# DMA transposes, 64-row tail matmuls, one merged broadcast and GpSimd weight loads in a fused attention and mixer kernel

## The chip, the cores and the metric

The kernel runs on one core of one Trainium2 chip. The metric is the device time of one execution in microseconds (us); lower is better. Times quoted for a kernel are medians of its runs. The median of the kernel before was 252.76 us in its three first runs. A profiled execution has a "span", which is about 2 us shorter than its time. TensorE's clock is granted by a throttle, so every run also has a mean granted clock (1.0 is full speed). A run more than 1.5% above the fastest of its kernel is called slow and is kept out of every ratio.

Engines are named as in the profile: PE is TensorE's matmul, PEld its weight load, DVE is VectorE, ACT ScalarE, POOL GpSimd, SP SyncE, and a "q" behind a name is that engine's queue of issued transfers.

## The reference

Two blocks follow each other over x of shape 1 x 2048 x 448, all in bf16. The first is sliding-window attention (16 heads of 28, a window of 8 keys at a distance of 2). The second mixes neighbouring tokens and ends in an MLP of width 1792.

```python
def _A_ref(x, wqkv, wo):                     # x is layernorm(x)
    q, k, v = split_heads(x @ wqkv)          # cut
    ...                                      # 8 keys at distance 2, softmax over them
    return o @ wo
def _B_ref(x, w1, w2, w3, w4):               # x is layernorm(h)
    h = _gelu(_layernorm(x) @ w1)
    hs = shifted_quarters(h) @ w2            # cut: four quarters shifted by -1, +1, -2, +2 tokens
    x1 = x + hs
    return x1 + _gelu(_layernorm(x1) @ w3) @ w4

h  = x + _A_ref(_layernorm(x), wqkv, wo)
h2 = h + _B_ref(_layernorm(h), w1, w2, w3, w4)
```

## The kernel before

A small scheduler takes a list of operations, works out the dependences, and gives each engine one fixed order. Within an engine that order is then kept, whatever happens at run time. The 2048 tokens are handled in four stages of 512. The phases of a stage are A1 (layernorm), QK, V, att (scores, exp, mask, values), WO, B1, B2, W3 and B3.

Every layernorm output (512 tokens x 448) has to be turned so that the 448 channels lie on partitions. TensorE does this in 16 transposes of 128 x 112, and a copy of 1024 columns per half brings the result back from PSUM:

```python
KC = 112                                     # 448 = 4 x 112
def transposes(ls, dst):
    for half in range(2):
        T = tile()
        for il in range(4):
            for cc in range(2):
                c = 2 * half + cc
                S.add("pe", "transpose", 64.0, out=T(...), in_=lntm[:, ls, il, c*KC:(c+1)*KC], identity=ident[:])
        copy(dst(half), T(...), 1024, 0.52)
```

A contraction over 448 channels is four passes of 112 rows. The largest is W3, 14 output tiles of 4 matmuls each:

```python
def phase_W3(g):
    ...
    transposes(ls, lambda half: actT[:, a, 2*half:2*half+2, :])
    for f in range(NF):                      # 14
        T = tile()
        for c in range(4):
            mm(T(...), w3_s[:, c, f*128:(f+1)*128], actT[:, a, c, :], c == 0, c == 3, 512)
        act(h3T[g % 2][:, f, :], T(...), ACT.Gelu_apprx_tanh, 512)
```

At the end of an attention stage the softmax sums are gathered, inverted, stored to a scratch in HBM and broadcast back. Each of four rows of 8 KB goes to 32 partitions. VectorE then multiplies four tiles, oT, by the result:

```python
def phase_att(t):
    ...                                      # scores, exp, masks, values -> osb
    for j in range(4):
        dma("zg%d_%d" % (par, j), zp[32*j:32*j+32, par, :], osb[32*j+28:32*j+29, ...])
    dve("reciprocal", 400, out=rzp[:, par, :], in_=zp[:, par, :])
    ...
    dma("zs%d" % par, zd..., rzp[:, par, :], 32768)
    for j in range(4):
        dma("zb%d" % j, rzb[32*j:32*j+32, :, :]..., bass.AP(rz_d, (4*t+j)*2048, [[0, 32], [1, 2048]]), 32*8192)
    for c in range(4):
        dve("tensor_tensor", 512, out=oT[:, par, c, :], in0=osb[:, par, c, :], in1=rzb[:, c, :], op=ALU.mult)
```

All weights are loaded on SyncE's queue at the start, and every normalisation runs on VectorE.

## Time and profile before

| | before |
|---|---|
| median time, four runs beside the changed kernel | 252.35 us |
| span of the profiled run | 250.6 us |
| TensorE busy | 224.6 us (90%) |
| first QK matmul starts | 10.4 us |
| last value matmul of attention starts | 105.0 us |
| last B1 matmul of the last stage starts | 141.9 us |
| last B3 matmul starts | 245.4 us |

These are lines from the profile page of the kernel before: the busy times of the engines; the busy tenths of TensorE, its granted clock in tenths and the DMA share in 40 slices of the span; the chain that ended last, by engine; and the broadcast's transfers with the size of each and the median time to landing.

```profile
PE 224.6 (90%) x1681; PEld 112.9 (45%) x1681; DVE 138.2 (55%) x306; ACT 120.7 (48%) x175; POOL 46.2 (18%) x71
...
PE   0799799999979998898995999899998999899992
...
PEclk9999659999965995589998899999999999999998
DMA  6999900070610052007000000000100000000111
...
PE 72%; DVE 16%; ACT 5%; POOL 2%; issue 2%; DVEq 0%
...
rzb<-rz_scratch SPq DMA_DIRECT2D x16, 256.0 KB, 4.4
```

TensorE is the limit: busy for 90% of the span, and 72% of the chain. Among its groups of instructions the 192 transposes are 18.8 us, with 11.2 us of idle just before them. The slices show the few places where it rests and its clock drops: the start and the starts of attention stages. The DMA row shows that nearly all loads happen in the first five slices (about 31 us); later there is only the traffic of the broadcasts and outputs.

The next lines are from the timeline of TensorE (start us, busy us, engine, line, operation, tiles, count). The first two make one batch of 16 transposes, and the last is one W3 group of 56 matmuls:

```profile
159.62 0.58 PE L1100 MATMUL ps<-ident,lntm 128*112 128x128 bf16 x6
160.90 0.77 PE L1100 MATMUL ps<-ident,lntm 128*112 128x128 bf16 x10 [0.70 <-DVE lntm L1100]
...
162.45 12.25 PE L1100 MATMUL ps<-actT,w_s 112*128 112x512 bf16 x56
```

With the wait in its middle this batch ends 2.05 us after it starts; a batch without a wait takes about 1.06 us. A W3 group takes 12.25 us, 0.22 us a matmul.

Finally, a line of VectorE's timeline: the four multiplies of the last attention stage, which use a broadcast that SyncE issued at 113.58 us:

```profile
123.49 2.49 DVE L1100 TENSOR_TENSOR oT<-arena,rzb 128x512 bf16<-128x512 f32 x4
```

### The profile page before, as it was taken

How to read it: one execution, taken by the hardware profiler on the slowest of the kernel's cores; microseconds unless marked ns; L12 is line 12 of the kernel's file. 1: busy time of each engine (PE TensorE's matmuls, PEld its weight loads, DVE VectorE, ACT ScalarE, POOL GpSimd, SP SyncE). 2: the span in 40 equal slices, each digit the busy share in tenths (PEclk: the TensorE clock that was granted, in tenths of full speed). 3: DMA queues.
4: the chain of work that ended last, by engine and by line, in shares of the span. 5: the costliest groups of instructions: out<-in, count | busy, mean ns of one | idle time of the engine just before them, and what ended most of it. 6: DMA issues, size and time to landing. Idle time of an engine off the chain costs nothing.

```text
span 250.6 us, 4082 instructions
## 1 busy us (share of the span) xinstructions
PE 224.6 (90%) x1681; PEld 112.9 (45%) x1681; DVE 138.2 (55%) x306; ACT 120.7 (48%) x175; POOL 46.2 (18%) x71
## 2 busy tenths in 40 slices
PE   0799799999979998898995999899998999899992
PEld 0336345645533556354544533533554345533550
DVE  7596862595785677877999602700385008700220
ACT  2468836896485649645422575166002740156000
POOL 8512200010031003003017200800016000710000
PEclk9999659999965995589998899999999999999998
DMA  6999900070610052007000000000100000000111
GB/s 164 291 222 232 275 12 5 8 171 5 146 29 0 8 131 44 3 7 173 0 1 3 0 0 0 21 18 0 36 15 25 0 16 23 20 18 0 42 39 42
DMA packets 11696, 14.07 MB, mean 56 GB/s; under 512 B 2136, under 2 KB 10712, under 8 KB 11160
## 3 DMA queue, kind: packets, MB, share of 16 engines
q1 hardware_dynamic: 11672, 13.75, 22.7%
q8 instruction: 15, 0.25, 0.4%
q14 instruction: 9, 0.07, 0.1%
HBM read 11.65 MB, written 1.97 MB: 54 GB/s over the span
## 4 chain that ended last, share of the span: by engine, by line
PE 72%; DVE 16%; ACT 5%; POOL 2%; issue 2%; DVEq 0%
PE ps L1100 72%; DVE st L1100 4%; DVE lntm L1100 4%; ACT pt L1100 3%; DVE xb L1100 2%; POOL rstd L1100 2%; DVE mv L1100 1%; DVE oT L1100 1%; ACT hT L1100 1%; ACT actT L1100 1%; DVE pt L1100 1%; ACT arena L1100 0%; POOL vtmp L1100 0%; DVE xin L1100 0%; DVE msk L1100 0%
## 5 line engine op out<-in xcount | busy, mean ns | idle before, releaser
L1100 PE MATMUL ps<-actT,w_s 112*128 112x512 bf16 (+1 forms) x288 | 64.2, 382 | 1.2 <-DVE mv L1100 1.1
L1100 ACT ACTIVATE arena<-ps 128x512 bf16<-128x512 f32 (+1 forms) x67 | 40.0, 597 | 28.0 <-PE ps L1100 27.8
L1100 PE MATMUL ps<-w_s,arena 128*128 128x448 bf16 x224 | 43.9, 353 | 0.0
L1100 PEld LDWEIGHTS ps<-actT,w_s 112*128 112x128 bf16 (+1 forms) x288 | 25.9, 106 | 37.8 <-ACT arena L1100 15.2
L1100 PE MATMUL ps<-hT,arena 112*128 112x512 bf16 x128 | 39.4, 453 | 0.5 <-ACT hT L1100 0.2
L1100 DVE TENSOR_TENSOR ost<-ps,xb 128x448 bf16<-128x448 f32 x16 | 10.0, 622 | 54.2 <-PE ps L1100 54.1
L1100 ACT ACTIVATE pt<-ps 110x1024 bf16<-110x1024 f32 x32 | 30.3, 1030 | 7.8 <-PE ps L1100 7.8
L1100 ACT ACTIVATE actT<-ps 112x1024 bf16<-112x1024 bf16 x10 | 10.0, 1028 | 44.2 <-PE ps L1100 44.2
L1100 POOL TENSOR_SCALAR vtmp<-mv 128x4 f32<-128x4 f32 (+1 forms) x19 | 4.6, 241 | 143.0 <-DVE mv L1100 142.3
L1100 PEld LDWEIGHTS ps<-w_s,arena 128*128 128x128 bf16 x224 | 21.5, 98 | 20.5 <-DVE xb L1100 0.6
L1100 PE MATMUL ps<-ident,lntm 128*112 128x128 bf16 x192 | 18.8, 250 | 11.2 <-DVE lntm L1100 11.2
L1100 PEld LDWEIGHTS ps<-ident,lntm 128*112 128x112 bf16 x192 | 15.9, 152 | 14.5 <-DVE lntm L1100 12.1
L1100 DVE TENSOR_TENSOR pt<-pt,msk 110x1024 bf16<-110x1024 bf16 x32 | 21.0, 684 | 1.7 <-ACT pt L1100 1.7
L1100 DVE BATCH_NORM_STATS2 st<-xin 128x6 f32<-128x448 bf16 x32 | 19.2, 601 | 2.4 <-DMA xin<-in_A_x_dram 1.9
L1100 PEld LDWEIGHTS ps<-hT,arena 112*128 112x128 bf16 x128 | 11.6, 108 | 17.9 <-issue 6.0
L1100 POOL TENSOR_TENSOR rstd<-vtmp,mhalf 128x4 f32<-128x4 f32 (+1 forms) x19 | 18.5, 972 | 1.6
L1100 POOL TENSOR_TENSOR xb<-xb,xin 128x448 bf16<-128x448 bf16 x16 | 16.7, 1072 | 1.5 <-DVE lntm L1100 1.5
L1100 DVE TENSOR_TENSOR xb<-ps,xb 128x448 bf16<-128x448 f32 x16 | 9.6, 600 | 13.4 <-PE ps L1100 13.1
L1100 PE MATMUL ps<-qT,kT 28*110 28x103 bf16 (+1 forms) x320 | 13.2, 229 | 3.8 <-ACT pt L1100 3.5
L1100 PE MATMUL ps<-wo_s,oT 128*128 128x448 bf16 x64 | 16.2, 403 | 0.4 <-DVE oT L1100 0.3
L1100 PE MATMUL ps<-arena,hT 112*110 112x448 bf16 x80 | 15.8, 353 | 0.0
L1100 ACT ACTIVATE gT<-ps 112x512 bf16<-112x512 f32 x16 | 9.6, 600 | 12.3 <-PE ps L1100 12.3
(52 smaller groups left out, 188.5 us busy)
## 6 DMA issues: line engine op xcount, KB each, us to landing
rzb<-rz_scratch SPq DMA_DIRECT2D x16, 256.0 KB, 4.4
w_s<-in_B_w_dram SPq DMA_DIRECT2D x2, 1568.0 KB, 18.0
out_dram<-ost SPq DMA_DIRECT2D x16, 112.0 KB, 1.7
xin<-in_A_x_dram SPq DMA_DIRECT2D x3, 448.0 KB, 8.9
arena<-in_A_wqkv_dram SPq DMA_DIRECT2D x3, 392.0 KB, 6.2
w_s<-in_B_w_dram SPq DMA_DIRECT2D x2, 392.0 KB, 10.5
xin<-in_A_x_dram SPq DMA_DIRECT2D x4, 112.0 KB, 2.2
wo_s<-in_A_wo_dram SPq DMA_DIRECT2D x4, 98.0 KB
```

The costliest lines, as they stand in the source:

```text
L1100: inst = getattr(eng, op.meth)(**op.kw)
```

## The change

The intent is to take work off TensorE: 11 of the 12 batches of transposes go to the DMA, and a contraction over 448 becomes three passes of 128 rows and one of 64, where the 64-row passes ("tails") of two output tiles use the two halves of the array side by side. To match this, layernorm outputs are padded to 512 columns (the last 64 repeated), and the last 64 rows of weights are loaded twice. Beside it, the four broadcast transfers are merged into one, the four gathers into one, the weights move to GpSimd's queue and are issued at two later points, the normalisations may run on VectorE or ScalarE (ScalarE needs a second quantity, nmr, made by two more GpSimd instructions), and some late phases change places. The diff, cut to its core:

```diff
+    def dmaw(chan, out_ap, in_ap, nbytes):
+        return S.add("pool", "dma_start", 1100.0, chan=chan, lat=nbytes, out=out_ap, in_=in_ap)
 ...
     def normalize(slot, kind, i, out_ap, in_ap):
-        S.add("dve", "tensor_scalar", 390, ...)
+        S.add("flex", "tensor_scalar", 0, ..., opts={"dve": ("tensor_scalar", ...), "act": ("activation", ...)})
 ...
+    def transpose_dma(ls, a, b, dst):
+        S.add("sp", "dma_start_transpose", 500.0, chan="tr%d_%d" % (ls, a), lat=(b - a) * 128 * 1024, out=dst,
+              in_=lntm[:, ls, a:b, :].rearrange("p i n -> p (i n)"))
+
+    def mm_k(outs, lhs, rhs, n):
+        for g, o in enumerate(outs):
+            for c in range(3):
+                mm(o, lhs(g, c, 0, 128), rhs(g, c, 0, 128), c == 0, False, n)
+        for g, o in enumerate(outs):
+            r = 64 * (g % 2)
+            S.add("pe", "matmul", n / 4.8 + 8, out=o, lhsT=lhs(g, 3, r, r + 64), rhs=rhs(g, 3, r, r + 64), start=False, stop=True)
 ...
-        for j in range(4):
-            dma("zb%d" % j, rzb[32 * j:32 * j + 32, :, :].rearrange("p c n -> p (c n)"),
-                bass.AP(rz_d, (4 * t + j) * 2048, [[0, 32], [1, 2048]]), 32 * 8192)
+        dma("zb", rzb[:].rearrange("p c n -> p (c n)"), bass.AP(rz_d, 4 * t * 2048, [[2048, 4], [0, 32], [1, 2048]]), 128 * 8192)
 ...
-        transposes(ls, lambda half: actT[:, a, 2 * half:2 * half + 2, :])
-        for f in range(NF):
-            T = tile()
-            for c in range(4):
-                mm(T(lambda p: p[:, 0, :]), w3_s[:, c, f * 128:(f + 1) * 128], actT[:, a, c, :], c == 0, c == 3, 512)
-            act(h3T[g % 2][:, f, :], T(lambda p: p[:, 0, :]), ACT.Gelu_apprx_tanh, 512)
+        transpose_dma(ls, 0, 4, actT[:, a, :, :, :].rearrange("p i c n -> p (i c) n"))
+        for f0 in range(0, NF, 2):
+            Ts = [tile(), tile()]
+            mm_k([T(lambda p: p[:, 0, :]) for T in Ts], ...)
+            for q, T in enumerate(Ts):
+                act(h3T[g % 2][:, f0 + q, :], T(lambda p: p[:, 0, :]), ACT.Gelu_apprx_tanh, 512)
 ...
+    behind(load_attn_out)        # after A1 1: w_o, w1, w2
 ...
+    behind(load_mlp)             # after A1 2: w3, w4
 ...
-    phase_WO(3)
     phase_B1(0)
     phase_B1(1)
     phase_B2(0)
+    phase_WO(3)
```

## The prediction

> **What bounds the kernel now.** TensorE. The page gives it 224.6 us of a 250.6 us span (90%), and 72% of the chain that ended last (VectorE 138.2, ScalarE 120.7). TensorE's idle 26 us lies in the first 7 us, in short waits at the start of attention stages (the timeline: 0.3 to 0.5 us before each group of score matmuls, for an exp), and at hand-overs of normalised tiles (the waits: 11.2 us for lntm, 7.0 of it the start). The granted clock is 0.57 to 0.59 in three stretches of 10 to 13 us after such waits.
>
> **Removed.** (1) 176 of 192 TensorE transposes. A batch of 16 takes about 1.06 us in the timeline, so 11 batches are 11.7 us, plus about 4 us of idle before them. (2) The half-row tails. A full 512-column matmul takes 0.218 us at full clock (26 in 5.78 us). If two 64-row tails run side by side, 3.5 passes for 4 save 28 of them in W3 (6.1 us), 8 in W1 (1.7), 16 in QK (3.5), and 8 narrower ones in V (1.5): 12.8 us. The trace supports this: 30 score matmuls of 28 rows and 103 columns on alternating row groups took 0.71 us, 24 ns each.
>
> Gross: 28 us, nearly all on the chain.
>
> **Added.** (a) A DMA transpose of 512 KB where a 1.06 us batch stood. At 261 GB/s (the Trainium skill, "DMA: Bandwidth & Descriptors", latency and other measured facts) this is 2 us; with the 1.9 us a small transfer here needs to land, and its issue, I estimate 5 to 6 us. No trace shows one yet. (b) Two more small GpSimd instructions per statistics step; in the first stage four steps are in series on the chain: about +2 us. (c) The reciprocal's broadcast becomes one 1 MB transfer instead of four of 256 KB (4.4 us to landing). Its source's outermost dimension is 4. The same page (how many engines) says such a transfer uses 4 engines. With 8 KB packets at 0.31 us or more that is 32 in a row: about 10 us, landing near 12 us (estimate).
>
> **Where the gain is lost.** After the last attention stage, reciprocal, store, broadcast (12 us) and four multiplies (2.5 us) make a chain of about 20 us to WO 3, while TensorE has some 10.5 us of other work: a wait of about 9 us. Then WO 3, statistics, transpose, B1 3: again up to 5 us. In attention, all four stages now start with 80 or more score and value matmuls without filler: one more cold stretch (about 5 us) and 3 to 4 us of waits, against 11 us saved. The final stretch (W3 and B3, 108.4 us in before) keeps its gain: about 13 to 14 us.
>
> Sum: start +2, attention -3, middle 0, end -13.
>
> **Predicted time:** 240 us, 228 to 252 in 8 of 10 cases. Faster by over 2%: 0.76; within 2%: 0.18; slower: 0.06.
>
> **What will show it.** TensorE busy near 200 us, W3 plus its tails near 10.7 us a group; transposes landing in 4 to 7 us; broadcast landing near 12 us; a wait of 5 to 10 us in front of WO 3; four cold stretches; first QK matmul near 12.3 us instead of 10.4.
>
> **What would make it wrong.** DMA transposes of 10 us or more each put waits before B1 and W3 and could cost all the gain. Tails that do not run side by side lose 12 us. If the broadcast still lands in 5 us, the time falls toward 232.

## The result, and the profile after

The changed kernel took 299.46 us in the median of four runs (298.64 to 303.14; the last of these is a slow run), against 252.35 us (251.75 to 252.82) before. The ratio is 1.186, with a 95% interval of 1.180 to 1.192: 47 us slower. A ratio is always the mean time of one kernel's fast runs over that of the other's fast runs in the same rounds, so it is not quite the ratio of the medians quoted.

The lines of the profile page and, for the two kinds of transpose, of the list of transfers, which answer to those shown of before:

```profile
PE 221.0 (74%) x1499; PEld 96.6 (33%) x1505; DVE 130.9 (44%) x289; ACT 122.0 (41%) x187; POOL 61.7 (21%) x121
...
PE   0596399890097909986596048699999999999992
...
PEclk9999589577569775966579659799999999999998
...
PE 45%; DMA 33%; DVE 10%; SPq 4%; POOL 3%; issue 2%; ACT 1%; POOLq 0%
...
rzb<-rz_scratch SPq DMA_DIRECT2D x4, 1024.0 KB
```

```profile
hT<-lntm SPq DMA_TRANSPOSE x12, 2.5
...
actT<-lntm SPq DMA_TRANSPOSE x8, 4.3
```

The chain that ended last is no longer TensorE's: its share fell from 72% to 45%, and DMA, which was absent, has 33%. The row of TensorE has holes of whole slices (each is 7.4 us) in the first 60% of the span, and its clock row has many more fives, sixes and sevens. The DMA transposes landed in 2.5 us (128 KB) and 4.3 us (512 KB), no slower than predicted. These are medians, counted from the start of the issue. One transpose of 20 was far slower: it was issued at 163.86 us, while the last broadcast was in flight, and took 9.5 us to issue and 11.6 us to land.

The waits of the changed kernel (who waited for whom: total us, times, longest us):

```profile
DVE oT L1167 <- DMA rzb<-rz_scratch: 45.4, 4, 17.2
...
PE ps L1167 <- DVE oT L1167: 18.9, 2, 13.3
...
PE ps L1167 <- DVE qT L1167: 14.9, 1, 14.9
...
PE ps L1167 <- DVE pt L1167: 9.2, 3, 8.5
```

VectorE waited for the broadcast in all four stages, 45.4 us together. TensorE then waited for VectorE: for oT, which needs the broadcast, but also for qT and pt, which do not. Waits of TensorE for DMA transposes are small beside these: 4.2 us once for hT and 2.2 us once for actT. The timeline of VectorE in the first attention stage shows why:

```profile
60.28 1.28 DVE L1167 TENSOR_TENSOR pt<-pt,msk 110x1024 bf16<-110x1024 bf16 x2
...
78.74 2.50 DVE L1167 TENSOR_TENSOR oT<-arena,rzb 128x512 bf16<-128x512 f32 x4 [17.18 <-DMA rzb<-rz_scratch]
81.16 0.68 DVE L1167 CAST qT<-ps 128x512 bf16<-128x512 f32 x1
```

VectorE's next operation in its order was oT, so it stood still for 17.18 us. The copy of qT, whose input was long there, sat behind it. TensorE needed the PSUM bank which that copy frees:

```profile
81.90 6.62 PE L1167 MATMUL ps<-arena,hT 128*110 128x448 bf16 x20 [14.95 <-DVE qT L1167]
```

The chain that ended last (start us, us, what) shows what the broadcast costs, from its issue to its use. These are its lines for the first and the last stage:

```profile
50.74 27.98 DMA rzb<-rz_scratch
78.74 2.50 DVE oT L1167 x4
...
156.25 17.45 DMA rzb<-rz_scratch
```

The two stages between have 17.81 and 18.64 us. That is 17.5 to 28 us from issue to use. In the kernel before, the four transfers together take 6.6 to 6.8 us from the first issue to the last landing (one alone 4.4 us in the median). In the last stage TensorE waited 13.28 us in front of WO 3, where the prediction had about 9:

```profile
174.47 5.76 PE L1167 MATMUL ps<-wo_s,oT 128*128 128x448 bf16 x16 [13.28 <-DVE oT L1167]
```

### The profile page after: what moved, and what is told of

Read it like the earlier page. It is cut to its first block, busy times and chain, and to the rows that moved or that the text cites. A ratio compares the mean times of both kernels' runs of the same rounds, so it can differ in the third digit from the quotient of the medians.

```text
span 296.8 us, 3753 instructions
## 1 busy us (share of the span) xinstructions
PE 221.0 (74%) x1499; PEld 96.6 (33%) x1505; DVE 130.9 (44%) x289; ACT 122.0 (41%) x187; POOL 61.7 (21%) x121
## 4 chain that ended last, share of the span: by engine, by line
PE 45%; DMA 33%; DVE 10%; SPq 4%; POOL 3%; issue 2%; ACT 1%; POOLq 0%
PE ps L1167 45%; DMA rzb<-rz_scratch 28%; SPq L1167 4%; DVE oT L1167 3%; DMA rz_scratch<-rzp 2%; DVE st L1167 2%; DMA actT<-lntm 1%; DMA hT<-lntm 1%; DVE lntm L1167 1%; POOL rstd L1167 1%; DVE xb L1167 1%; POOL nmr L1167 1%; ACT lntm L1167 1%; POOL msk L1167 1%; DVE mv L1167 1%
## 5 line engine op out<-in xcount | busy, mean ns | idle before, releaser
L1167 PE MATMUL ps<-actT,w_s 128*128 128x512 bf16 (+3 forms) x288 | 68.2, 405 | 2.8 <-DMA actT<-lntm 2.2
L1167 ACT ACTIVATE arena<-ps 128x512 bf16<-128x512 f32 (+1 forms) x67 | 37.0, 595 | 59.8 <-PE ps L1167 59.7
L1167 PE MATMUL ps<-hT,arena 128*128 128x512 bf16 (+1 forms) x122 | 36.4, 463 | 5.5 <-DMA hT<-lntm 4.2
L1167 PEld LDWEIGHTS ps<-actT,w_s 128*128 128x128 bf16 (+3 forms) x288 | 24.6, 108 | 44.9 <-issue 25.8
L1167 PE MATMUL ps<-wo_s,oT 128*128 128x448 bf16 x64 | 18.6, 442 | 19.1 <-DVE oT L1167 18.9
L1167 PE MATMUL ps<-arena,hT 128*110 128x448 bf16 (+1 forms) x80 | 19.5, 406 | 14.9 <-DVE qT L1167 14.9
L1167 DVE TENSOR_TENSOR oT<-arena,rzb 128x512 bf16<-128x512 f32 x16 | 10.0, 687 | 45.4 <-DMA rzb<-rz_scratch 45.4
L1167 PEld LDWEIGHTS ps<-hT,arena 128*128 128x128 bf16 (+1 forms) x128 | 10.4, 105 | 24.4 <-issue 13.2
L1167 PE MATMUL ps<-qT,kT 28*110 28x103 bf16 (+1 forms) x320 | 13.8, 236 | 5.9 <-ACT pt L1167 5.6
L1167 PE MATMUL ps<-pt,vt 110*32 110x103 bf16 (+1 forms) x320 | 9.9, 263 | 10.4 <-DVE pt L1167 8.9
L1167 PEld LDWEIGHTS ps<-arena,hT 128*110 128x110 bf16 (+1 forms) x80 | 9.1, 140 | 25.4 <-DVE qT L1167 15.2
```

The costliest lines, as they stand in the source:

```text
L1167: inst = getattr(eng, op.meth)(**op.kw)
```

## The experiments

Theories A to C stood at the outset for the 47 us. Theory D was added after the first four runs, for what was left:

- A: the merged broadcast runs on few engines and its lateness blocks VectorE's queue in every stage.
- B: the DMA transposes, with their small packets, slow every other transfer.
- C: the weight loads, now on GpSimd's queue and in the middle of attention, slow every other transfer.
- D: the 64-row tails do not save what they should.

All experiments are judged by ratio to the fast runs of the unchanged kernel before on the same chip. The batches ran on different chips, so two experiments are compared by these ratios.

| experiment | median us | ratio to before (95%) |
|---|---|---|
| e1: after, broadcast in four transfers | 258.08 | 1.025 (1.018 to 1.032) |
| e2: before, broadcast in one transfer | 287.59 | 1.136 (1.127 to 1.146) |
| e3: after, one transfer with 16 rows outermost | 264.05 | 1.046 (1.039 to 1.054) |
| e4: after, one transfer with 8 rows outermost | 271.91 | one run |
| f1: e1, tails of a pair on the same rows | 265.92 | 1.054 (1.047 to 1.061) |
| f2: e1, tails four by four in W1 and W3 | 252.62 | 0.999 (0.994 to 1.004) |
| f3: e1, four full passes instead of tails | 248.99 | 0.984 (0.978 to 0.989) |
| f5: e1, full-row tails in the same order | 256.90 | 1.020 (1.013 to 1.026) |
| g1: e1, all transposes on TensorE | 251.60 | 0.994 (0.987 to 1.001) |
| h1: e1, weights on SyncE's queue | 256.25 | 1.007 (1.000 to 1.015) |
| h2: e1, normalise on VectorE only | 255.15 | 1.011 (1.003 to 1.019) |
| c1: f3 and g1 together | 253.97 | 1.010 (1.005 to 1.015) |
| b1: f3, but W3 as in f2 | 254.23 | 1.014 (1.005 to 1.023) |
| b2: b1 with an early start as before | 247.82 | 0.988 (0.980 to 0.995) |
| b5: before with late changes only | 243.01 | 0.968 (0.959 to 0.976) |

Where a median includes slow runs (h1 above all, two of four), the ratio is the better guide.

### Is it the broadcast? e1, e2, e3, e4

**e1** is the changed kernel with the one broadcast issued as the four transfers of before, at the same place and with the same semaphore. The order of operations on every engine is the same as in the changed kernel (the traces agree; SyncE alone has more issues).

```diff
-dma("zb", rzb[:]..., bass.AP(rz_d, 4*t*2048, [[2048, 4], [0, 32], [1, 2048]]), 128*8192)
+for j in range(4):        # one entry for the scheduler, four transfers when emitted
+    dma(rzb[32*j:32*j+32, :, :]..., bass.AP(rz_d, (4*t + j)*2048, [[0, 32], [1, 2048]]))
```

> The changed kernel with only the reciprocal's broadcast split again into four transfers of 256 KB (each with an outermost source dimension of 32); every engine's order stays as in the changed kernel. Theory A (the 1 MB transfer runs on 4 DMA engines because its outermost source dimension is 4, and the multiplies that need it block VectorE's in-order queue): landing falls from 17 to 28 us to 5 to 7 us, VectorE's 45 us of waiting for it nearly vanish, the time falls to 232 to 248 us. Theory B (the new transposes, 23552 packets of 256 B on the same queue, slow the broadcast) and theory C (the weights on the GpSimd queue slow it): the bytes and the company are the same, so landing stays above 12 us and the time above 285 us.

Measured: 258.08 us, so this one split takes back 41 of the 47 us (1.186/1.025 is 1.157). The rest is still slower than before, and the absolute time came out above the range that my theory gave it. A line of its waits, to be compared with that of the changed kernel above:

```profile
DVE oT L1171 <- DMA rzb<-rz_scratch: 3.9, 2, 3.1
```

VectorE's wait for the broadcast went from 45.4 to 3.9 us, and in the same view TensorE's waits for qT and for pt fell from 14.9 and 9.2 us to 0.9 and 0.3. Theories B and C cannot explain the 41 us, since transposes and weight loads are untouched here.

**e2** is the counterpart: the kernel before with nothing but the merge. Only SyncE's list of issues changes.

```diff
-for j in range(4):
-    dma("zb%d" % j, rzb[32*j:32*j+32, :, :]..., bass.AP(rz_d, (4*t+j)*2048, [[0, 32], [1, 2048]]), 32*8192)
+dma("zb", rzb[:]..., bass.AP(rz_d, 4*t*2048, [[2048, 4], [0, 32], [1, 2048]]), 128*8192)
```

> The kernel before with only its four broadcast transfers made one of 1 MB with an outermost source dimension of 4; no DMA transpose, no weight on the GpSimd queue, same order on TensorE, VectorE, ScalarE and GpSimd. Theory A: landing 15 to 19 us, about 4 packets of 8 KB in flight, the time rises by 25 to 45 us to 278 to 298 us. Theories B and C: landing stays near 5 us and the time within 2% of before.

Measured: 1.136 in fast runs, 34 us slower than before. Neither a transpose on the DMA nor a moved weight load is in this kernel. The wait of VectorE (the profiled run was a slow one, so its absolute times are not compared closely):

```profile
DVE oT L1098 <- DMA rzb<-rz_scratch: 39.3, 4, 11.6
```

**e3 and e4** keep one transfer of 1 MB, but change the size of the source's outermost dimension. The scratch gets four (e3) or two (e4) copies of each row, and the broadcast reads 16 rows for 8 partitions each, or 8 rows for 16 each.

```diff
-dma("zs%d" % par, zd..., rzp[:, par, :], 32768)
-dma("zb", rzb[:]..., bass.AP(rz_d, 4*t*2048, [[2048, 4], [0, 32], [1, 2048]]), 128*8192)
+for u in range(4):                                   # e4: 2
+    dma(bass.AP(rz_d, (16*t + u)*2048, [[8192, 4], [64, 32], [1, 64]]), rzp[:, par, :])
+dma("zb", rzb[:]..., bass.AP(rz_d, 16*t*2048, [[2048, 16], [0, 8], [1, 2048]]), 128*8192)   # e4: [2048, 8], [0, 16]
```

> The changed kernel with the broadcast still one transfer of 1 MB, but the scratch holds every reciprocal row four times, so that the outermost source dimension is 16 (four small stores of 32 KB instead of one). Theory A: about 16 packets in flight, landing 5 to 7 us, time within 2% of the run with four transfers (232 to 250 us). If instead merging into one instruction is what hurts: landing stays near 17 us and the time near 295 us.

> As the 16-row run but every row twice: outermost source dimension 8. Theory A: about 8 packets in flight, landing 8 to 10 us, time between the 16-row run and the changed kernel, 240 to 265 us. If the engine count is not what matters: landing near 17 us or near 5 us as the other runs, not between.

Measured: 264.05 us with 16 rows and 271.91 us with 8. Both are above their expected ranges, but their order is right: the more rows outermost, the faster. VectorE's wait, first for e3, then for e4:

```profile
DVE oT L1171 <- DMA rzb<-rz_scratch: 9.8, 3, 9.3
```

```profile
DVE oT L1171 <- DMA rzb<-rz_scratch: 21.8, 4, 11.5
```

The trace also has every 8 KB packet of these transfers. For each of the four stages, in order, the mean number of packets in flight and the time from the first to the end of the last packet, worked out from the 128 packets of SyncE's queue that follow each issue:

| kernel | outermost rows | in flight | us from first to last packet |
|---|---|---|---|
| before (four transfers) | 32 each | 14.2, 14.8, 14.9, 15.0 | 5.0, 4.8, 4.9, 5.1 |
| after | 4 | 2.7, 3.9, 3.7, 3.7 | 22.8, 15.9, 16.7, 15.5 |
| e2 | 4 | 3.5, 3.8, 3.7, 3.7 | 16.6, 16.4, 18.2, 16.8 |
| e4 | 8 | 5.8, 7.6, 7.5, 8.1 | 12.2, 9.0, 9.6, 9.4 |
| e3 | 16 | 13.8, 14.7, 14.7, 15.3 | 5.3, 4.9, 4.9, 5.3 |
| e1 (four transfers) | 32 each | 8.2, 14.9, 14.9, 14.8 | 8.8, 5.0, 5.0, 5.1 |

Four rows outermost give on average up to 4 packets in flight, 8 give about 8, 16 give about 15. The Trainium skill says this in "DMA: Bandwidth & Descriptors", section "Why a DMA increments its semaphore by 16 and not by 1": a transfer goes to the largest number of engines, up to 16, that divides the slowest dimension of both access patterns. The trace agrees, with 3.9 in flight on average at most for 4 rows (6 for moments). Theory A is shown: the same merge of four transfers into one costs 41 us with 4 rows outermost, but with 16 rows the broadcast is as quick as four transfers.

What remains beside it lies in the first stage. Four weight loads were issued there on GpSimd's queue, between 49.6 and 53.8 us in after, e1, e3 and e4. The first broadcast of e1 takes 8.8 us, and the first packets of those of after, e1 and e4 come 4 to 5 us after the issue, against 0.9 to 1.4 us in their later stages. In e3 the broadcast itself takes 5.3 us, but it was issued only at 64.7 us, behind four small stores issued at 50.2 to 52.0 us, for which SyncE waited 12.2 us; the longest wait of e3, 9.3 us, is in this stage. These runs alone do not say why; the weights loaded at that time are a likely reason (see h1 and b1).

### What do the 64-row tails save? f1, f2, f3, f5

All of these start from e1.

**f1** lets both tails of a pair use the same 64 rows (in V, W1 and W3), so that they have to run one after the other.

```diff
-            r = 64 * (g % 2)
+            r = 0                    # V, W1, W3; QK as it was
```

> The changed kernel with the four broadcast transfers, and with every 64-row tail matmul of V, W1 and W3 on rows 0 to 63 (before, the two of a pair used rows 0 to 63 and 64 to 127). Same order on all engines, same result. Theory D (the tails of a pair do run side by side, 4 ns apart, but the switches from 128 rows to 64 and back each expose a weight load of about 0.1 us, so the pair costs as much as two full passes): the tails now run one after the other, so a group of 56 W3 matmuls goes from 12.1 us to 17 or 18 us if each tail costs a further 0.2 us, and the kernel gets 6 to 10 us slower. Theory E (the tails never overlapped): no change, 12.1 us a group, time within 1% of the run with four transfers.

**f2** takes four tiles at once in W1 and W3, so that two pairs of tails follow each other and a W3 group of 14 tiles changes between 128 and 64 rows and back 4 times instead of 7.

```diff
-        for f0 in range(0, NF, 2):
-            Ts = [tile(), tile()]
+        for f0 in range(0, NF, 4):
+            Ts = [tile() for _ in range(min(4, NF - f0))]      # W1: one group of four
```

> The changed kernel with the four broadcast transfers and W1 and W3 computed in groups of four tiles (twelve full passes, then four tails) instead of two, so that there are half as many switches. Theory D: about 0.2 us less per four tiles, a group of 56 W3 matmuls falls from 12.1 us to 11.3 to 11.6 us, the kernel 2 to 4 us faster than with pairs (254 to 256 us). Theory E: 12.1 us stays.

**f3** gives up tails: every tile gets four full passes of 128 rows, with the second half of the last chunk of weights set to zero.

```diff
-            for c in range(3):
-                mm(o, lhs(g, c, 0, 128), rhs(g, c, 0, 128), c == 0, False, n)
-        for g, o in enumerate(outs):
-            r = 64 * (g % 2)
-            S.add("pe", "matmul", n / 4.8 + 8, ..., start=False, stop=True)
+            for c in range(4):
+                mm(o, lhs(g, c, 0, 128), rhs(g, c, 0, 128), c == 0, c == 3, n)
```

> The changed kernel with the four broadcast transfers and four full passes of 128 rows (the last chunk's rows 64 to 127 of the weights are zero) instead of three and a half: undoes that part of the change on TensorE. Theory D: a W3 group takes 12.0 to 12.2 us as with the tails, and the time is within 1% of the run with four transfers (255 to 261 us). My prediction on record, that the half passes save 12.8 us, would have this kernel at about 270 us.

**f5** makes the tails 128 rows deep at the very places where the 64-row tails stood (QK keeps its 64 rows), with the order of e1 on every engine. Its result is wrong (relative error 0.31), since the last 64 channels are then counted twice.

```diff
-            r = 64 * (g % 2)
-            S.add(..., lhsT=lhs(g, 3, r, r + 64), rhs=rhs(g, 3, r, r + 64), ...)
+            r, k = (0, 128)          # V, W1, W3
+            S.add(..., lhsT=lhs(g, 3, r, r + k), rhs=rhs(g, 3, r, r + k), ...)
```

> The changed kernel with the four broadcast transfers, with the last chunk's matmuls of V, W1 and W3 as full 128-row passes in the same places; every engine's order stays exactly as in the run with four transfers. The result is wrong on purpose (the last 64 rows count twice), the work is that of four full passes. Theory D (the half-row pairs save next to nothing because of the two switches): within 1% of the run with four transfers, 256 to 260 us, a W3 group 11.85 us start to start against 11.74. Then the 9 us that the kernel with four full passes gained came from the order and from tiles finishing one at a time, not from the matmuls. If full passes are themselves what is faster: 248 to 251 us.

Measured: the timeline of TensorE has one W3 group in each of e1, f1, f2 and f3, in this order. The kernel before had 12.25 us for the same group.

```profile
178.61 12.12 PE L1171 MATMUL ps<-actT,w_s 128*128 128x512 bf16 x56 [0.51 <-DVE ost L1171]
```

```profile
181.60 13.60 PE L1171 MATMUL ps<-actT,w_s 128*128 128x512 bf16 x56 [0.49 <-DVE ost L1171]
```

```profile
175.41 11.48 PE L1171 MATMUL ps<-actT,w_s 128*128 128x512 bf16 x56 [0.52 <-DVE ost L1171]
```

```profile
170.31 12.25 PE L1173 MATMUL ps<-actT,w_s 128*128 128x512 bf16 x56 [0.52 <-DVE ost L1173]
```

Three and a half passes cost 12.12 us, four full ones 12.25 us. Predicted were 10.7. In f1 the group grew by 1.48 us, which is 7 tails of 0.21 us, so in e1 the tails of a pair do run side by side. (My expectation of 17 to 18 us for that group had the size wrong.) The saving is lost around them. The single records of one pair in e1, from the trace (start us, ns, what):

```
182.915 379 MATMUL     128 rows
183.131 379 MATMUL     128 rows      the last full pass, 0.216 after the one before
183.439  92 LDWEIGHTS   64 rows
183.442  92 LDWEIGHTS   64 rows
183.443 386 MATMUL      64 rows      0.312 after the last full pass
183.446 386 MATMUL      64 rows      0.003 after its partner
183.760  96 LDWEIGHTS  128 rows
183.765 390 MATMUL     128 rows      0.319 after the tails
183.991 379 MATMUL     128 rows      0.226 after that
```

The second tail starts 3 ns after the first. But the step into the tails takes 0.312 us and the step out of them 0.319, where a step between full passes takes about 0.22. The other pairs of W3 in e1 agree: 0.311 or 0.312 us in, 3 or 4 ns between the tails, 0.318 or 0.319 us out, with three steps that were longer. From the start of the last full pass to that of the next one it is 0.634 us. With two full passes in place of the pair, these would be three steps of 0.216, or 0.648 us (worked out). In the timeline of the weight loads in e1 the same is seen as a gap labelled "issue" before both:

```profile
181.19 0.10 PEld L1171 LDWEIGHTS ps<-actT,w_s 128*128 128x128 bf16 x1
181.72 0.10 PEld L1171 LDWEIGHTS ps<-actT,w_s 64*128 64x128 bf16 x2 [0.42 <-issue]
182.04 0.55 PEld L1171 LDWEIGHTS ps<-actT,w_s 128*128 128x128 bf16 x4 [0.23 <-issue]
```

The 64-row weights are loaded only 0.308 us after the last full pass has started, and the next 128-row weights 0.314 us after the tails. Between full passes the loads hide under the running matmuls. The Trainium skill, "TensorE: Matmul & The Clock Gate", section "Part 3: Packing small matmuls — row/col tiling", gives about 4 ns from one packed tile to the next, and says that the load of a tile is pulled ahead of running matmuls where the row groups do not conflict. The first agrees with these records: 3 ns between the tails. The second only in part: no load was early where a half and the full array follow each other, but full passes use the same rows too and their loads are early (the section also names a background weight buffer). Why the switch stops the early load is not shown here. f2 has 3 switches in and out fewer a group and gains 0.64 us, 0.21 us each: this is the same cost again, seen from the other side. As a kernel f2 is some 6 us faster than e1 (0.999 against 1.025), more than its expectation of 2 to 4 us and more than the 2.6 us of four W3 groups; what else it gains is open, as with f3.

Now the surprise: f3, whose matmuls are no cheaper, is 9 us faster than e1, and f5, which keeps e1's order, is only some 1 us faster. So f3's gain hardly comes from the matmuls of V, W1 and W3. QK, which f5 left at 64 rows, is no cheaper in f3 either where it can be compared: the 32 QK matmuls of the first stage take 7.88 us from the first start to the last in e1 and 8.29 us in f3. What is left is what the two differ in otherwise: the places and the pairing of the tiles. In f3 each tile ends by itself and its copy can start, and the scheduler arranges all engines anew. Which of these it is, and how much belongs to the tail loads of weights that f3 also drops, is left open.

### The DMA transposes: g1, c1

**g1** is e1 with all transposes back on TensorE, writing the layout of the changed kernel. **c1** is g1 and f3 together.

```diff
-        transpose_dma(ls, 0, 4, actT[:, a, :, :, :].rearrange("p i c n -> p (i c) n"))
+        transposes(ls, lambda half: actT[:, a, :, 2*half:2*half+2, :].rearrange("p i c n -> p c i n"))
```

> The changed kernel with the four broadcast transfers and all transposes back on TensorE (with the 512-column layout and the half-row tails). If the DMA transposes are a gain (my prediction: 11.7 us of TensorE work and some 4 us of idle saved), this is 8 to 14 us slower than the run with four transfers, 266 to 272 us. If the waits they bring (4.5 us at the first, 2.3 us before B1 3, and the cold clock after them) eat that gain, it is within 1.5%, 254 to 262 us.

> The changed kernel with the four broadcast transfers, four full passes and all transposes on TensorE: what is left of the change is the order of the phases, the GpSimd queue and the choice of engine for normalising. If the two undone parts each cost what they showed alone (9 us and 6.5 us) and add up: 240 to 246 us. If both only disturb the same schedule: 247 to 253 us, as each alone or as before. If the rest of the change is worth nothing or harms: 252 to 258 us.

Measured: g1 0.994, faster than both of its expected ranges. So in e1's surroundings the kernel is 3% slower with the DMA transposes than without (1.025/0.994), though they take 11 batches from TensorE; g1's order is the scheduler's own as well, so the 3% are not the transposes' alone. c1 is 1.010: the two gains over e1, 3% from g1 and 4% from f3, do not add but cancel in part. This is in the last of its three expected ranges, and it suggests that a part's worth depends on the order that the scheduler makes around it. Why TensorE does not profit is plain in one place. The transpose is longer than what it replaces, and where the next matmul needs it at once, TensorE waits. A line of the TensorE timeline of e1, at the first matmul of the second stage:

```profile
36.01 0.63 PE L1171 MATMUL ps<-hT,arena 128*128 128x512 bf16 x1 [4.53 <-DMA hT<-lntm]
```

Four transposes of 128 KB are issued in series, each about 1.27 us (5.27 us for the four in the changed kernel, from 26.93 us on), and then the last lands. TensorE waited 4.5 us for them. In the kernel before one batch took 1.06 us. This one wait is shown; what the other transposes cost or save in e1 was not separated.

### Weights and normalisation: h1, h2

**h1** is e1 with the weights on SyncE's queue, at the same points of the program. **h2** is e1 with normalisation on VectorE alone and without the two extra GpSimd instructions.

```diff
     def dmaw(chan, out_ap, in_ap, nbytes):
-        return S.add("pool", "dma_start", 1100.0, chan=chan, lat=nbytes, out=out_ap, in_=in_ap)
+        return S.add("sp", "dma_start", 500.0, chan=chan, lat=nbytes, out=out_ap, in_=in_ap)
```

> The changed kernel with the four broadcast transfers and the weight loads issued on the SyncE queue instead of the GpSimd queue, at the same points of the program. GpSimd loses 8.5 us of issuing between the statistics of the third and fourth stage. If the GpSimd queue costs nothing on the chain: within 1.5%, 254 to 262 us; if its loads delay statistics or share the broadcast's time (the first broadcast took 12.5 us beside them, the others 5), up to 6 us faster, 251 to 255 us.

```diff
-        pool("tensor_scalar", 60, out=nmr..., scalar1=-1.0, ...)
-        pool("tensor_tensor", 60, out=nmr..., in1=rstd..., op=ALU.mult)
 ...
-        S.add("flex", "tensor_scalar", 0, ..., opts={"dve": ..., "act": ...})
+        S.add("dve", "tensor_scalar", 390, ..., op0=ALU.subtract, op1=ALU.mult)
```

> The changed kernel with the four broadcast transfers, normalising on VectorE alone and without the two extra GpSimd instructions per statistics step. The first QK matmul comes 2 to 2.5 us earlier (10.4 us as in before, against 12.8). If that is all: 254 to 257 us. If ScalarE's normalises (0.75 us where VectorE takes 0.39) and the GpSimd steps also sit on later chains: 248 to 254 us.

Measured: h1 1.007 and h2 1.011, against e1's 1.025. Both seem to undo a part of what was left, 1.8% and 1.4%; h1 rests on two fast runs, and h2's interval touches that of e1. The profiled runs of both were slow ones, so only the ratios are used, and one plain reading: in h2 the first QK matmul starts at 10.6 us (12.8 in e1, 10.4 before). That the place of the weight loads, in the middle of attention, costs something is likely but was not isolated: no run has them at the start again with the rest of the change kept.

### Toward a faster kernel: b1, b2, b5

**b1** is f3, but W3 keeps 64-row tails in groups of four, as in f2. **b2** is b1 with the first two stages transposed on TensorE, and the first stage normalised without nmr.

```diff
-        for f0 in range(0, NF, 2):                 # f3
-            Ts = [tile(), tile()]; mm_k(...)
+        for f0 in range(0, NF, 4):                 # b1
+            Ts = [tile() for _ in range(min(4, NF - f0))]; mm_half(...)
 ...
-        if t == 0:                                 # b1
+        if t <= 1:                                 # b2
             transposes(...)
```

> The changed kernel with the four broadcast transfers, full passes for QK, V and W1, and half-row tails only in W3 in groups of four tiles. The kernel with full passes everywhere had 0.984 of the time before; this should take 2.6 us off (11.10 for 11.87 us a group), 244 to 249 us. If the pairing of tiles hurts in W3 as well: 249 to 254 us.

> As b1, with the second stage's transposes on TensorE too (the first DMA transpose made TensorE wait 4.5 us) and without the extra GpSimd steps in the first stage. If these two are the costs of the attention part: first QK matmul at 10.5 us, no wait for hT, 4 to 6 us faster than b1, 239 to 245 us. If the gain is taken by other waits in the attention stages: within 2 us of b1.

Measured: b1 1.014, slower than f3 instead of faster: a miss. Its W3 groups did take the 11.10 us of f2 (from the start of the first to that of the last matmul; f3 has 11.88). But the timeline of VectorE shows a wait in attention that f3 did not have in this size (its longest was 2.15 us):

```profile
51.38 0.55 DVE L1181 RECIPROCAL rzp<-zp 128x64 f32<-128x64 f32 x1 [9.29 <-DMA zp<-arena]
```

This is the gather of 32 KB of softmax sums, issued at 41.37 us. Eleven weight loads had been issued between 30.7 and 38.4 us (in f3 ten, between 25.2 and 32.4 us). All but one of them landed before the gather did, at 33.5 to 48.9 us; that it had to wait for them is likely, not shown. b2 then gives 0.988, no better than f3 and above its expected range. Its first QK matmul starts at 11.95 us (b1: 13.31), later than expected, and that gather still keeps VectorE for 7.06 us. Where the rest of its gain over b1 lies was not worked out.

**b5** goes the other way. It starts from the kernel before and changes only the late part, where every stage of work has another to hide behind: DMA transposes for W3 1 to 3 (W3 0 stays on TensorE), W3 with 64-row tails in groups of four, and the late phases in another order. Attention, loads and broadcast are those of before.

```diff
+            S.add("sp", "dma_start_transpose", 1900.0, ..., out=actW[:, a]..., in_=lntm[:, ls]...)    # g > 0
+        for f0 in range(0, NF, 4):
+            fs = range(f0, min(f0 + 4, NF)); Ts = [tile() for _ in fs]
+            ...                                    # three passes of 128 rows for each tile, then the 64-row tails
     phase_B2(1)
+    phase_B2(2)
     phase_W3(1)
     phase_B3(0)
-    phase_B2(2)
+    phase_B2(3)
     phase_W3(2)
```

> The kernel before up to B1 3, and from there: the transposes of W3 1, 2 and 3 by DMA, W3 in groups of four tiles with half-row tails, and the order of phases of the changed kernel. If DMA transposes are a gain where a stage of 10 us or more lies before their use: three batches of 1.06 us, three waits of 0.7 us and 4 x 0.65 us of W3 go, about 8 us, 243 to 247 us. If a DMA transpose costs as much as it saves even there: 248 to 252 us.

Measured: 243.01 us, a ratio of 0.968 (0.959 to 0.976): faster than both kernels. The results are correct. The busy times on its page:

```profile
PE 216.8 (90%) x1633; PEld 108.1 (45%) x1633; DVE 139.8 (58%) x308; ACT 112.4 (46%) x171; POOL 45.7 (19%) x71
```

TensorE is busy 7.8 us less than before, with the same share of the span. Of that, 3.2 us are the three batches of transposes (3 x 1.06), and 3.1 us are the W3 groups (4 x (11.87 - 11.10)). So two of the ideas of the change take work off TensorE where there is slack and few switches, and no wait of TensorE for a DMA transpose is in its trace. But b5 changes three things at once: how its 8 us divide among transposes, tails and order is not shown.

## Why the prediction was wrong

The direction was wrong: 240 us predicted, 299.46 measured. The parts, in the order of the prediction:

**TensorE bounds the kernel, and 28 us can be taken from it.** The first half held; the second was half right. The transposes: 11 batches of 1.06 us, 11.7 us, are indeed gone. Busy time in e1 (214.6 us) is 10.0 us below that of before (224.6), which is about that term alone. The predicted 200 us needed the tails' 12.8 us as well.

**The half-row tails save 12.8 us.** This term was mis-sized; it is about nil as the change makes the tails. The prediction took them for free if the pair runs side by side, and supported it with score matmuls of 28 rows (24 ns each). They do run side by side, 3 ns apart, but each change between 128 and 64 rows costs about 0.1 us, twice a pair. A W3 group went from 12.25 to 12.12 us, not to 10.7. The score matmuls could not have shown this: they never switch to full rows in the middle of their run.

**(a) The DMA transposes.** The size was nearly right: 5 to 6 us estimated for 512 KB, and 4.3 us measured in the median, which includes 1.3 to 1.9 us of issuing (one took 11.6 us, beside the last broadcast). 128 KB took 2.5 us. The 261 GB/s of the Trainium skill ("DMA: Bandwidth & Descriptors", "Latency and other measured facts"; for a middle dimension that is not contiguous) agrees with the trace in order: 384 KB more take 1.8 us more, about 218 GB/s. What was missed is that a TensorE wait of 4.2 us follows in the second stage, where there is no work to hide it.

**(b) Two microseconds at the start.** Right: the first QK matmul at 12.8 us instead of 10.4, 12.3 predicted. h2 takes 2.2 us of it back (10.6 us), by undoing the two GpSimd instructions and the normalising on ScalarE together; which of the two it is was not separated.

**(c) The merged broadcast lands near 12 us, and costs only a wait before WO 3.** This is the step that failed, twice over. The mechanism of few engines was right, with 2.7 to 3.9 packets in flight on average, as the skill has it. But 32 packets one after another took 15.5 to 22.8 us, not 10: a packet took 380 to 480 ns (median), more than the assumed 310, and fewer than four were in flight on average. From issue to use it was 17.5 to 28 us. Worse, I charged it only where its result is needed last, at WO 3 (about 9 us, 13.28 measured), and charged the other three stages nothing for it. The multiplies that use the broadcast stand in VectorE's order in each of the four stages, ahead of masks and copies that TensorE needs. The Trainium skill, "TensorE: Matmul & The Clock Gate", "Architectural detail: the array is 16× 32×32, not 1× 128×128", says that VectorE's queue is strictly first in, first out; the trace agrees, as VectorE stood for 17.18 us in front of a copy of qT whose input was there. The lateness, some 11 to 21 us over the 6.6 to 6.8 us of before, was paid in every stage: 45.4 us of waits of VectorE. e1 and e2 show it from both sides, 41 us taken back by the split alone, 34 us lost by the merge alone.

**Four cold stretches.** Counted as the prediction counted (10 us or longer), there were seven; before has three, and e1, with the broadcast split, has the four that were predicted. The clock records, which begin 13 to 16 us into the span, give half speed in stretches of 3.4 to 17.1 us. Up to the last matmul they sum to 88.7 us in the changed kernel (nine stretches), 51.2 us in e1 (six), and 37.5 us in before (four). The Trainium skill, "TensorE: Matmul & The Clock Gate", "Part 1: The HAM clock gate (the "warmup" mystery)", describes the state after an idle window of about 3.4 us as half clock. The trace agrees in part. All these stretches are whole multiples of 3.4 us (3.4, 6.8, 10.2, 13.7, 17.1). In the changed kernel four of them, 51.2 us, begin after a window of 3.4 us in which TensorE was busy for 0 to 17%, in gaps of 5.6 to 14.9 us. But the three long ones of before follow windows in which it was busy for 55 to 74%, with no gap over 0.7 us. So a long wait of VectorE can be paid for twice: in TensorE's idle time and in its slower clock after it. This agrees with TensorE's busy time: 221.0 us in the changed kernel and 214.6 in e1, with the same 1499 matmul records in the same order.

**"Start +2, attention -3, middle 0, end -13".** With the broadcast split again (e1), the profiled span is 5.4 us longer than that of before. I cut the span where the same matmul starts in both kernels. The window of attention, from the start of the first QK matmul to that of the last value matmul, first in before, then in e1 (columns: window, its us, then busy us of PE, PEld, DVE, ACT and POOL with their instructions, the granted clock, the DMA share and GB/s):

```profile
10.40:105.00 94.60, 87.88 (x951) 46.22 (x950) 66.08 (x139) 64.50 (x90) 11.28 (x18) 0.84 0.40 93
```

```profile
12.80:112.20 99.40, 85.58 (x893) 39.80 (x899) 69.38 (x145) 59.45 (x84) 26.29 (x44) 0.83 0.43 104
```

The start is +2.4 us, as predicted. Attention is +4.8 us instead of -3: TensorE's busy time fell by only 2.3 us, and its idle time grew. The middle, to the last B1 matmul of the last stage, is 44.2 us against 36.9, +7.3. 19 W3 matmuls run early there and leave the end. At full clock they would be 4.1 us (estimate, 19 x 0.216), so the middle is +3.2; most of these 3.2 us is the clock, as the 19 take 7.0 us there, most of it at half clock. To the last B3 matmul the end is 94.2 us against 103.5, and with those 4.1 us it is -5.2 instead of -13. That is what the three late batches (3.2 us) and the waits around them (3 x 0.70 us) come to. Nothing is left for the tails, which is what f1 to f3 say too.

**The conditions named for being wrong.** Slow transposes, tails in series, a fast broadcast: none of these occurred, but for one transpose of 11.6 us. A broadcast much slower than 12 us was not on the list, though its duration was the least certain estimate. "If the broadcast still lands in 5 us, the time falls toward 232" was tried by e1, and failed by 26 us, for the reasons above.

Left open: what f3 gains by its order, why gains do not add (c1), what weights in the middle of attention cost, what parts b5 gains by, and how much of the 41 us is the half clock (TensorE's busy time accounts for 6.4 us of it).

## What to carry to other kernels

Before merging small transfers, look at the outermost dimension of the merged access pattern, as it decided here how many packets were in flight (4, 8 and 16 rows); and charge a late transfer not where its result is needed but where its first user stands in an engine's fixed order, with everything behind it. The 64-row matmuls saved next to nothing where the array had to change its row shape before and after each pair (12.12 us against 12.25); in groups of four they took 11.48: group them, or fill the rows. Put a DMA transpose where a stage of other work lies between it and its user: in b5 no TensorE wait for one is recorded, in e1 the first user waited 4.5 us.

## What the Trainium skill lacked or had wrong

- "DMA: Bandwidth & Descriptors", "Rules for kernel authors": the rows that advise one large transfer in place of several small ones stand without the condition that another row of the same table has. Here one transfer of 1 MB, with 4 rows outermost, had 2.7 to 3.9 packets in flight and took 15.5 to 22.8 us; four of 256 KB had 14 to 15 in flight and took 4.8 to 5.1 us (before). The merge alone made the kernel 34 us slower (e2). The rule on the outermost dimension itself agrees with the runs at 4, 8 and 16 rows.
- "DMA: Bandwidth & Descriptors", "DMA Transpose (X-bar)": the page has a bandwidth, in another section, but no time for one transpose of this kind between on-chip tiles on Trainium2. Here 128 KB took about 1.27 us to issue and 2.5 us to land, counted from the start of the issue; 512 KB took 1.3 to 1.9 us and 4.3 us.
- "TensorE: Matmul & The Clock Gate", "Part 3: Packing small matmuls — row/col tiling": the speedups are for packed matmuls among themselves. The time that a change between full-height and half-height matmuls costs is missing. "TensorEngine Tiling (Array Packing)", "Key Properties", does say that a change of tiling mode drains TensorE, but gives no figure. Here it was 0.312 us into the pair and 0.319 us out of it, against 0.216 us between full passes, so that three and a half passes cost 12.12 us where four cost 12.25.
- "TensorE: Matmul & The Clock Gate", "Part 1: The HAM clock gate (the "warmup" mystery)": it ties half clock to an idle window of about 3.4 us. In the kernel before, the three long half-clock stretches began with TensorE busy for 55 to 74% of the 3.4 us before, and with no gap over 0.7 us.
